# The prologue of a fused sketch-attention and feed-forward kernel: load order, k features and dummy matmuls rearranged

## The chip, the cores and the metric

The kernel runs on one core of a Trainium2 chip. The metric is the time of one execution on the device, in microseconds (us). The core has a matrix engine (TensorE, PE in the profile, with PEld for its weight loads), a vector engine (VectorE, DVE), an activation engine (ScalarE, ACT), a general engine (GpSimd, POOL) and a queue engine (SyncE, SP). DMA transfers are issued from SP's and ACT's queues here and run on 16 DMA engines. SBUF is the memory on the core; PSUM is the accumulator that TensorE writes.

## What is computed

Four batches of 1088 tokens with 4 heads of 32 go through a linear attention whose features are products of two small sketches, and the result through a feed-forward layer with a squared ReLU:

```python
def phi(x):                                   # S1, S2: 8 x 32
    a = np.einsum('rd,bhsd->bhsr', S1, x)
    b = np.einsum('rd,bhsd->bhsr', S2, x)
    return np.einsum('bhsi,bhsj->bhsij', a, b).reshape(*x.shape[:-1], r * r)   # 64 features
q_p, k_p = (phi(q), phi(k))
kv = np.einsum('bhsf,bhsd->bhfd', k_p, v)
z = np.sum(k_p, axis=2)
num = np.einsum('bhsf,bhfd->bhsd', q_p, kv)
den = np.einsum('bhsf,bhf->bhs', q_p, z)[..., None] + 1e-06
x = (num / den)                               # -> [4352 tokens, 128]
h = np.maximum(x @ w_in, 0.0)                 # 128 -> 2048
out = h * h @ w_out                           # 2048 -> 128
```

## The kernel before

The feed-forward layer works on stretches of 256 to 448 tokens of one batch. For each of the 16 blocks of 128 hidden features, TensorE makes `pg` (L562: w_in block by xT), ACT takes the ReLU `gt` (L571), ACT or VectorE squares it to `g` (L579, L581), and TensorE adds it into `po` (L600). The attention of the later stretches and batches is worked out in between. All of that, from the first `pg` on, is put in order by a planner (class `_Order`, with costs and due times): the costs and due times are fixed numbers in the code, and each engine runs its instructions in the planned order.

What stands ahead of the first `pg` is an order written out by hand, the prologue. It makes x for the first 256 columns of batch 0 (8 of the 34 token blocks of each head), for which it needs kv and z over all of batch 0's keys. Its steps, with their lines before:

- Loads. ACT's queue issues S1 and S2 into `s_nat` (L200, L201) and then v's parts 2 and 3; SP's queue issues k in two parts (token blocks 0 to 3 and 4 to 8 of each group, L164), the first 256 columns of q (L170), v's parts 0 and 1 (L177), and then w_in (L186), the rest of q and w_out (L191) in pieces. A v part fills 32 of the 128 partitions. A semaphore is shared by every eighth transfer, so the ninth waits until the first has landed.
- Dummies. `keep_warm(n)` (L633) issues n matmuls of 128x512 on constants into a tile that nobody reads. W0 to W5 are the counts at six places: 12, 2, 2, 2, 1, 1.
- Small constants. POOL makes `iden` (an identity, in a helper), `irep` (L238, four copies of parts of it), zeros in `vn` and `z`; VectorE makes `own_c`, `own_p` and zeros.
- Sketch matrices. VectorE transposes `s_nat` to `s_T` (L646); four copies by ACT and POOL put it block by block into `sf` (L648), others into `sq` (L650 to L657) and into further columns of `sf` (L684), which only the planned part reads.
- k features. VectorE transposes k in blocks of 32x32 to `kT` (L270). TensorE makes `kf` with the sketch in `sf` as the stationary operand and tokens moving (L294). The result has features on the partitions, so VectorE transposes it back to `fs` (L303), and then takes the products `kp` (L314).
- q features. `qT` (L276), four matmuls with `sq` into `x0` (L678), a copy `qb0` (ACT) and the product `qp0` (L694).
- kv. `kvp` (L368): 36 small matmuls (9 token blocks by 4 heads), accumulated in one PSUM tile, whose stationary operand is `kp` and whose moving operand is v and a column of ones. float32 matmuls show as two passes each.
- The end: `bd` (L701, masked kv), `den0` and `num0` (L718), and on VectorE `dT`, `dn`, `rd`, `bc` and `xT` (L725 to L735); beside that the copies of kv for the later stretches (`kvt`, `irep`, L411, L417). POOL casts w_in in four pieces of 512 columns (L710) for `pg`.

TensorE, VectorE, ACT and POOL each run their own instructions strictly in the order of the code, and so does each DMA queue.

Of the kernel before, what the change touches and what calls it, by code (L numbers as in the profile page):

```python
# [9 lines left out]
F32 = mybir.dt.float32  # L10
# [85 lines left out]
def kernel(  # L96
# [11 lines left out]
    nc = tc.nc  # L108
# [4 lines left out]
    SP = 128 * NT  # L113
# [4 lines left out]
    W0, W1, W2, W3, W4, W5 = 12, 2, 2, 2, 1, 1  # L118
# [24 lines left out]
    def sb(name, cols, dt=F32, rows=128):  # L143
        return cpool.tile([rows, cols], dt, tag=name, name=name)
# [24 lines left out]
    def load_q(eng, b, c0, c1):  # L169
        eng.dma_start(  # L170
            qn[b % 2][:, c0:c1],
            bass.AP(q.tensor, q.offset + b * H * S * D + c0, [[G * D, 128], [1, c1 - c0]]),
        )
# [28 lines left out]
    load_k(nc.sync, 0, 0, 4)  # L202
    load_k(nc.sync, 0, 4, 5)
# [3 lines left out]
    load_q(nc.sync, 0, 0, 256)  # L207
    load_v(nc.sync, 0, 0)
    load_v(nc.scalar, 0, 2)
    load_v(nc.sync, 0, 1)  # L210
    load_v(nc.scalar, 0, 3)
# [11 lines left out]
    iden = sb("iden", 128)  # L223
    make_identity(nc, iden[:])
# [5 lines left out]
    own_c, own_p, irep = sb("own_c", 32), sb("own_p", 2), sb("irep", 128)  # L230
# [4 lines left out]
    for h in range(H):  # L235
        r = slice(32 * h, 32 * h + 32)
        nc.vector.memset(own_c[r, 8 * h : 8 * h + 8], 1.0)
        nc.gpsimd.tensor_copy(  # L238
            _ap(irep, 32 * h, 32, 0, [[32, 4], [1, 32]]),
            _ap(iden, 32 * h, 32, 32 * h, [[0, 4], [1, 32]]),  # L240
        )

    nc.vector.memset(kT[:, S:SP], 0.0)
    nc.vector.memset(qT[:, S:SP], 0.0)
    for i in range(2):
        nc.gpsimd.memset(_ap(vn[i], 96, 32, 32 * (NT - 2), [[32 * NT, H], [1, 64]]), 0.0)
    nc.gpsimd.memset(vn[0][:, VC : VC + 32], 1.0)
    nc.gpsimd.memset(zs[1][:], 0.0)
    ones = vn[0][:, VC : VC + 32]
# [18 lines left out]
    def a_kT0(t0, n):  # L268
        p = 3 if t0 + n > NT - 2 else 4
        nc.vector.transpose(  # L270
            _ap(kT, 0, 128, 32 * t0, [[32 * NT, p], [1, 32 * n]]),
            _ap(kn[0], 0, 128, 32 * t0, [[32 * NT, p], [1, 32 * n]]),
        )
# [16 lines left out]
    def a_kf(t0, n, pool, tag):  # L290
        kf = pool.tile([128, 512], F32, tag=tag, name="kf")
        for x in range(2):
            for p in range(4):
                nc.tensor.matmul(  # L294
                    kf[32 * p : 32 * p + 32, 32 * n * x : 32 * n * x + 32 * n],
                    sf[:, 32 * x : 32 * x + 32],
                    kT[:, 32 * (NT * p + t0) : 32 * (NT * p + t0 + n)],
                )
        st["kf", t0] = kf

    def a_fs(t0, n):
        fs = wpool.tile([128, 64 * n], F32, tag="fs0", bufs=2, name="fs0")
        nc.vector.transpose(fs[:, :], st["kf", t0][:, 0 : 64 * n])  # L303
        st["fs0", t0] = fs
# [5 lines left out]
    def a_kp0(t0, n, g0, gn):  # L310

        fs = st["fs0", g0]
        o = 32 * (t0 - g0)
        nc.vector.tensor_tensor(  # L314
            out=_ap(st[0, "kp"], 0, 128, 256 * t0, [[64, 4 * n], [8, 8], [1, 8]]),
            in0=_ap(fs, 0, 128, o, [[8, 4 * n], [1, 8], [0, 8]]),
            in1=_ap(fs, 0, 128, o + 32 * gn, [[8, 4 * n], [0, 8], [1, 8]]),
            op=mult,
        )
# [325 lines left out]
    a_kT0(0, 4)  # L645
    nc.vector.transpose(s_T[:, :], s_nat[:, :])  # L646
    for h, eng in enumerate((nc.scalar.copy, nc.gpsimd.tensor_copy, nc.scalar.copy, nc.gpsimd.tensor_copy)):
        eng(_ap(sf, 32 * h, 32, 8 * h, [[32, 2], [1, 8]]), _ap(s_T, 0, 32, 0, [[8, 2], [1, 8]]))  # L648
    a_kf(0, 4, psf, "po")
# [6 lines left out]
    for h, eng in ((1, nc.scalar.copy), (2, nc.gpsimd.tensor_copy), (3, nc.scalar.copy)):  # L656
        eng(  # L657
            _ap(sq, 32 * h, 32, 64 * (h % 2), [[128, 2], [1, 64]]),
            _ap(sq, 0, 32, 0, [[128, 2], [1, 64]]),
        )  # L660
    a_kT0(4, 3)
    a_kT0(7, 2)
    a_qT(0, 0, 8)
    keep_warm(W1)
    a_kf(4, 5, psf, "po")
    a_fs(0, 4)
    new_kp(0)
    a_kp0(0, 4, 0, 4)
    a_fs(4, 5)
    a_kp0(4, 3, 4, 5)  # L670
    a_kp0(7, 2, 4, 5)
# [3 lines left out]
    for x in range(2):  # L675
        for y in range(2):
            r, o = slice(64 * y, 64 * y + 64), 512 * (2 * x + y)
            nc.tensor.matmul(x0[:, o : o + 256], sq[r, 128 * x : 128 * x + 128], qT[r, 0:256])  # L678
    qb0 = wpool.tile([128, 512], F32, tag="qb0", bufs=1, name="qb0")
    qp0 = wpool.tile([128, 512], F32, tag="qp0", bufs=1, name="qp0")  # L680
    nc.scalar.copy(_ap(qb0, 0, 128, 0, [[256, 2], [1, 256]]), banks(x0, 0, 0, 256))
    for h in range(H):
        eng = (nc.scalar.copy, nc.gpsimd.tensor_copy)[h % 2]
        eng(sf[32 * h : 32 * h + 32, 64:96], s_T[:, :])  # L684
    keep_warm(W2)
    st[0, "kvp"] = psf.tile([128, 512], F32, tag="pg", name="kvp")
    for t0, n in ((0, 4), (4, 3), (7, 2)):
        for t in range(t0, t0 + n):
            a_kv0(t)
        if t0 == 0:  # L690
            keep_warm(W3)
        elif t0 == 4:
            keep_warm(W4)
# [14 lines left out]
    nc.scalar.copy(st["kvt"][:, :], st[0, "kvp"][:, 0:128])  # L708
    for c in range(4):
        nc.gpsimd.tensor_copy(  # L710
            w_in[:, 512 * c : 512 * c + 512], w_in32[:, 512 * c : 512 * c + 512]
        )
    keep_warm(W5)
# [265 lines left out]
```

## Time and profile before

| | us |
|---|---|
| median of 5 runs | 197.35 (197.01 to 197.8) |
| the profiled execution | 197.2 |
| its span in the profile | 195.4 |
| first `pg` (start of the feed-forward stage) | 16.80 from the span's start |
| first `kvp` on TensorE | 10.18 |
| POOL's casts of w_in start | 9.39, 10.49, 12.82, 14.17 |

The profile is of one execution. Its times are counted from the span's start. "Idle before" is the time that the engine stood still just before an instruction, with what ended it. A line like `L314 DVE TENSOR_TENSOR kp<-fs 128x768` names the line of the code, the engine, the operation, the tile written and read, and the shape.

### The profile page before, as it was taken

The page shows a single profiled execution, that of the slowest core. Times are in us where ns is not written, and L with a number is a line of the kernel's source. Part 1 is how long each engine was busy: PE and PEld are TensorE (multiplying, and loading weights), DVE is VectorE, ACT ScalarE, POOL GpSimd, SP SyncE. Part 2 cuts the span into 40 slices and gives each one's busy share as a digit, 9 for nine tenths or more (in the row PEclk, how much of TensorE's full clock was granted, in tenths as well). Part 3 has the DMA queues.
Part 4 walks back from the last instruction along what each step waited for, and adds up shares of the span by engine and source line. Part 5 has one row for each costly group of instructions (what it writes and reads, how often), then busy time and mean ns, then how long its engine had stood idle before and what let it go on. Part 6 is the DMA issues. An engine that isn't in the chain of part 4 may idle for free.

```text
span 195.4 us, 4341 instructions
## 1 busy us (share of the span) xinstructions
PE 185.7 (95%) x1700; PEld 123.1 (63%) x1700; DVE 112.9 (58%) x253; ACT 147.1 (75%) x323; POOL 26.8 (14%) x121
## 2 busy tenths in 40 slices
PE   8796999999999999999999999999999999999990
PEld 2363676656656656756677667566677665666890
DVE  3768659983948569579462896694832322333300
ACT  3305887975958979779499897785899998888950
POOL 6240000004900000082000001940000000000000
PEclk9999999999999999999999999999999999999999
DMA  6999200010039220020018610020020010020200
GB/s 175 265 373 269 48 0 5 0 30 3 0 47 248 91 47 0 3 42 3 0 20 198 171 34 3 0 40 3 0 36 7 16 19 2 9 38 3 36 5 27
DMA packets 24604, 11.32 MB, mean 58 GB/s; under 512 B 17672, under 2 KB 23176, under 8 KB 24584
## 3 DMA queue, kind: packets, MB, share of 16 engines
q1 hardware_dynamic: 24132, 10.72, 22.4%
q10 hardware_dynamic: 452, 0.33, 0.7%
q8 instruction: 13, 0.21, 0.4%
q14 instruction: 7, 0.06, 0.1%
HBM read 8.82 MB, written 2.23 MB: 57 GB/s over the span
## 4 chain that ended last, share of the span: by engine, by line
PE 89%; DMA 3%; DVE 2%; ACT 2%; issue 1%; SPq 0%; DVEq 0%
PE po L600 56%; PE pg L562 17%; PE nd L484 3%; DMA qn<-in_q_dram 3%; PE nd L493 2%; PE kvp L386 2%; PE pol L595 2%; PE po L595 2%; PE kvp L368 1%; PE qc L283 1%; PE kc L283 1%; ACT gt L571 1%; ACT g L579 1%; DVE kp L314 1%; SPq L164 0%
## 5 line engine op out<-in xcount | busy, mean ns | idle before, releaser
L600 PE MATMUL po<-g,w_o 128*128 128x384 f32 (+3 forms) x352 | 137.3, 475 | 0.0
L562 PE MATMUL pg<-xT,w_in 128*128 128x384 f32 (+3 forms) x192 | 108.9, 575 | 1.9 <-DVE xT L735 1.2
L571 ACT ACTIVATE gt<-pg 128x384 f32<-128x384 f32 (+4 forms) x177 | 85.4, 490 | 27.0 <-PE pg L562 25.2
L600 PEld LDWEIGHTS po<-g,w_o 128*128 128x128 f32 x352 | 62.8, 189 | 20.1 <-issue 5.1
L579 ACT ACTIVATE g<-gt 128x384 f32<-128x384 f32 (+4 forms) x133 | 68.7, 530 | 2.9
L562 PEld LDWEIGHTS pg<-xT,w_in 128*128 128x128 f32 x192 | 35.8, 189 | 27.6 <-issue 7.3
L581 DVE TENSOR_TENSOR g<-gt 128x384 f32<-128x384 f32 (+3 forms) x44 | 24.5, 557 | 35.9 <-ACT gt L571 35.7
L435 POOL COPY kv<-kvt 32x64 f32<-32x64 f32 x48 | 12.4, 259 | 94.4 <-DVE kvt L404 92.5
L452 DVE STREAM_SHUFFLE qa<-qc 128x576 f32<-128x576 f32 (+2 forms) x20 | 11.7, 650 | 0.0
L467 DVE TENSOR_TENSOR qp<-qa,qb 128x576 f32<-128x576 f32 (+2 forms) x20 | 10.9, 604 | 0.0
L439 POOL COPY z<-kvt 32x16 f32<-32x16 f32 x48 | 10.1, 209 | 0.0
L604 DVE STREAM_TRANSPOSE oT<-po 128x384 f32<-128x384 f32 (+3 forms) x11 | 6.2, 566 | 4.0 <-PE po L600 4.0
L339 DVE TENSOR_TENSOR kp<-fs 128x576 f32<-128x576 f32 x12 | 8.5, 740 | 0.0
L509 DVE STREAM_TRANSPOSE dT<-nd 128x128 f32<-128x128 f32 (+2 forms) x8 | 2.2, 309 | 10.0 <-PE nd L493 10.0
L636 PE MATMUL warm<-const-bfloat16-1.0 128*128 128x512 bf16 x20 | 6.7, 462 | 0.8 <-PEq L963 0.8
L484 PE MATMUL nd<-qp,kv 32*32 32x288 f32 (+2 forms) x320 | 6.8, 353 | 0.0
L330 DVE STREAM_TRANSPOSE fs<-kc 128x576 f32<-128x576 f32 x6 | 4.3, 762 | 3.9 <-PE kc L283 3.9
L276 DVE STREAM_TRANSPOSE qT<-qn 128x576 f32<-128x576 f32 (+4 forms) x10 | 5.7, 607 | 1.4 <-DMA qn<-in_q_dram 1.4
L595 PE MATMUL pol<-w_o,g 128*128 128x128 f32 x32 | 6.2, 275 | 0.0
L595 PE MATMUL po<-w_o,g 128*128 128x128 f32 x32 | 6.2, 274 | 0.0
L484 PEld LDWEIGHTS nd<-qp,kv 32*32 32x32 f32 x320 | 3.8, 103 | 3.5 <-issue 2.1
L452 DVE STREAM_SHUFFLE qb<-qc 128x576 f32<-128x576 f32 (+2 forms) x10 | 6.0, 645 | 0.0
(83 smaller groups left out, 97.7 us busy)
## 6 DMA issues: line engine op xcount, KB each, us to landing
kn<-in_k_dram SPq DMA_DIRECT2D x3, 544.0 KB
qn<-in_q_dram SPq DMA_DIRECT2D x3, 544.0 KB, 7.7
vn<-in_v_dram SPq DMA_DIRECT2D x11, 144.0 KB, 6.1
out_dram<-oT SPq DMA_DIRECT2D x24, 48.0 KB, 1.8
w_in<-in_moe_w_in_dram SPq DMA_DIRECT2D x4, 256.0 KB, 5.0
w_o<-in_moe_w_out_dram SPq DMA_DIRECT2D x4, 256.0 KB, 5.1
out_dram<-oT SPq DMA_DIRECT2D x8, 56.0 KB, 1.8
qn<-in_q_dram SPq DMA_DIRECT2D x1, 416.0 KB, 6.7
```

The lines of the kernel that those rows point to most:

```text
L339: nc.vector.tensor_tensor(out=_ap(st[b, "kp"], 0, 128, 2 * o, [[64, NT], [8, 8], [1, 8]]), in0=_ap(fs, 0, 128, o, [[32, NT], [1, 8], [0, 8]]),
L435: nc.gpsimd.tensor_copy(_ap(st[b, "kv"], 32 * c, 32, 64 * h, [[32, E], [1, 32]]), _ap(st["kvt"], 32 * h, 32, 0, [[64, E], [1, 32]]),)
L439: nc.gpsimd.tensor_copy(_ap(zs[b % 2], 32 * c, 32, 64 * h + 8 * c, [[32, E], [1, 8]]), _ap(st["kvt"], 32 * h, 32, 32, [[64, E], [1, 8]]),)
L452: nc.vector.stream_shuffle(in_=banks(st[b, "qc", i0], 2 * x, 0, m), out=_ap(st[b, which, i0], 0, 128, 2 * m * x, [[m, 2], [1, m]]), mask=m ...
L467: nc.vector.tensor_tensor(out=st[b, "qp", i0, e][:, r], in0=st[b, f"qa{e}", i0][:, r], in1=st[b, "qb", i0][:, r], op=mult,)
L484: nc.tensor.matmul(nd[32 * h : 32 * h + 32, 512 * c + col : 512 * c + col + m], kv[r, o : o + 32], qp[r, m * h : m * h + m], start=(e == 0 ...
L562: nc.tensor.matmul(st["pg", u][:, n * i : n * i + n], w_in[:, 128 * (d0 + i) : 128 * (d0 + i) + 128], st[b, "xT"][:, c0 : c0 + n],)
L571: nc.scalar.activation(gt[:, 0:w], st["pg", u][:, 0:w], Relu)
L579: nc.scalar.activation(g2[:, 0:w], gt[:, 0:w], Square)
L581: nc.vector.tensor_tensor(out=g2[:, 0:w], in0=gt[:, 0:w], in1=gt[:, 0:w], op=mult)
L595: nc.tensor.matmul(po[x // 128][:, 0:128], g[:, x : x + 128], w, start=(d == 0), stop=(d == NB - 1),)
L600: nc.tensor.matmul(po[0][:, 0:n], w, g, start=(d == 0), stop=(d == NB - 1))
```

## The change

k's transpose now goes into a tile `kt0` of its own, in an order in which 128 tokens (one block of 32 from each of four groups) are neighbours; `kf` is made with these tokens as the stationary operand and `sf` (64 columns) moving, so that tokens come out on the partitions. ACT copies the second half of `kf` to `kb`, and the product `kp` reads the first half from PSUM and `kb` from SBUF. q's first columns are loaded between the two parts of k, and v's four parts all go into SP's queue. `s_T` is made ahead of `kt0`; its copies into `sf` are all POOL's. `iden`, `irep` and some zeros are made behind these copies. The q sketch matmuls stand between the k feature matmuls. The dummies are 11 at the start and none elsewhere. A copy of one column of `kp` on POOL stands ahead of the casts of w_in.

```diff
--- before.py
+++ after.py
@@ -115,7 +115,7 @@
     NB = 16
     GT, G2, LA = 4, 6, 3.5
     LU = 4
-    W0, W1, W2, W3, W4, W5 = 12, 2, 2, 2, 1, 1
+    W0, W1 = 11, 0
 
 
 
@@ -200,15 +200,13 @@
     nc.scalar.dma_start(s_nat[0:8, :], S1[:, :])
     nc.scalar.dma_start(s_nat[8:16, :], S2[:, :])
     load_k(nc.sync, 0, 0, 4)
+    load_q(nc.sync, 0, 0, 256)
     load_k(nc.sync, 0, 4, 5)
 
     zero_a = sb("zero_a", 8)
     nc.scalar.copy(zero_a[:, :], nc.const_aps.tensor(0.0, (128, 8), F32))
-    load_q(nc.sync, 0, 0, 256)
-    load_v(nc.sync, 0, 0)
-    load_v(nc.scalar, 0, 2)
-    load_v(nc.sync, 0, 1)
-    load_v(nc.scalar, 0, 3)
+    for p in range(4):
+        load_v(nc.sync, 0, p)
     load_wi(nc.sync, 0)
     load_wi(nc.sync, 1)
     load_q(nc.sync, 0, 256, S)
@@ -220,33 +218,26 @@
     load_wo(nc.sync, 3)
 
 
-    iden = sb("iden", 128)
-    make_identity(nc, iden[:])
 
 
     sf, sq = sb("sf", 96), sb("sq", 256)
     nc.vector.memset(sf[:, 0:64], 0.0)
     nc.gpsimd.memset(sq[:], 0.0)
-    own_c, own_p, irep = sb("own_c", 32), sb("own_p", 2), sb("irep", 128)
+    nc.gpsimd.memset(_ap(vn[0], 96, 32, 32 * (NT - 2), [[32 * NT, H], [1, 64]]), 0.0)
+    nc.gpsimd.memset(vn[0][:, VC : VC + 32], 1.0)
+    ones = vn[0][:, VC : VC + 32]
+
+    kt0 = sb("kt0", SP)
+    nc.vector.memset(_ap(kt0, 0, 128, 128 * (NT - 2) + 96, [[128, 2], [1, 32]]), 0.0)
+    own_c, own_p = sb("own_c", 32), sb("own_p", 2)
     nc.vector.memset(own_c[:], 0.0)
     nc.vector.memset(own_p[:], 0.0)
     for i in range(2):
         nc.vector.memset(own_p[64 * i : 64 * i + 64, i : i + 1], 1.0)
     for h in range(H):
-        r = slice(32 * h, 32 * h + 32)
-        nc.vector.memset(own_c[r, 8 * h : 8 * h + 8], 1.0)
-        nc.gpsimd.tensor_copy(
-            _ap(irep, 32 * h, 32, 0, [[32, 4], [1, 32]]),
-            _ap(iden, 32 * h, 32, 32 * h, [[0, 4], [1, 32]]),
-        )
-
+        nc.vector.memset(own_c[32 * h : 32 * h + 32, 8 * h : 8 * h + 8], 1.0)
     nc.vector.memset(kT[:, S:SP], 0.0)
     nc.vector.memset(qT[:, S:SP], 0.0)
-    for i in range(2):
-        nc.gpsimd.memset(_ap(vn[i], 96, 32, 32 * (NT - 2), [[32 * NT, H], [1, 64]]), 0.0)
-    nc.gpsimd.memset(vn[0][:, VC : VC + 32], 1.0)
-    nc.gpsimd.memset(zs[1][:], 0.0)
-    ones = vn[0][:, VC : VC + 32]
 
     mask_a = [[4 * e + l // 8 for l in range(32)] for e in range(E)]
     mask_b = [8 + l % 8 for l in range(32)]
@@ -268,8 +259,8 @@
     def a_kT0(t0, n):
         p = 3 if t0 + n > NT - 2 else 4
         nc.vector.transpose(
-            _ap(kT, 0, 128, 32 * t0, [[32 * NT, p], [1, 32 * n]]),
-            _ap(kn[0], 0, 128, 32 * t0, [[32 * NT, p], [1, 32 * n]]),
+            _ap(kt0, 0, 128, 128 * t0, [[32, p], [128, n], [1, 32]]),
+            _ap(kn[0], 0, 128, 32 * t0, [[32 * NT, p], [32, n], [1, 32]]),
         )
 
     def a_qT(b, i0, n):
@@ -289,32 +280,27 @@
 
     def a_kf(t0, n, pool, tag):
         kf = pool.tile([128, 512], F32, tag=tag, name="kf")
-        for x in range(2):
-            for p in range(4):
-                nc.tensor.matmul(
-                    kf[32 * p : 32 * p + 32, 32 * n * x : 32 * n * x + 32 * n],
-                    sf[:, 32 * x : 32 * x + 32],
-                    kT[:, 32 * (NT * p + t0) : 32 * (NT * p + t0 + n)],
-                )
-        st["kf", t0] = kf
-
-    def a_fs(t0, n):
-        fs = wpool.tile([128, 64 * n], F32, tag="fs0", bufs=2, name="fs0")
-        nc.vector.transpose(fs[:, :], st["kf", t0][:, 0 : 64 * n])
-        st["fs0", t0] = fs
+        for t in range(n):
+            nc.tensor.matmul(
+                _ap(kf, 0, 128, 32 * t, [[32 * n, 2], [1, 32]]),
+                kt0[:, 128 * (t0 + t) : 128 * (t0 + t) + 128],
+                sf[:, 0:64],
+            )
+        kb = wpool.tile([128, 32 * n], F32, tag="kb", bufs=3, name="kb")
+        nc.scalar.copy(kb[:, :], kf[:, 32 * n : 64 * n])
+        st["kf", t0] = kf, kb
 
     def new_kp(b):
 
         st[b, "kp"] = wpool.tile([128, 64 * NT * H], F32, tag="kp", name="kp")
 
-    def a_kp0(t0, n, g0, gn):
-
-        fs = st["fs0", g0]
-        o = 32 * (t0 - g0)
+    def a_kp0(t0, n):
+
+        kf, kb = st["kf", t0]
         nc.vector.tensor_tensor(
             out=_ap(st[0, "kp"], 0, 128, 256 * t0, [[64, 4 * n], [8, 8], [1, 8]]),
-            in0=_ap(fs, 0, 128, o, [[8, 4 * n], [1, 8], [0, 8]]),
-            in1=_ap(fs, 0, 128, o + 32 * gn, [[8, 4 * n], [0, 8], [1, 8]]),
+            in0=_ap(kf, 0, 128, 0, [[8, 4 * n], [1, 8], [0, 8]]),
+            in1=_ap(kb, 0, 128, 0, [[8, 4 * n], [0, 8], [1, 8]]),
             op=mult,
         )
 
@@ -642,11 +628,11 @@
 
     st["warm"] = psf.tile([128, 512], F32, tag="pg", name="warm")
     keep_warm(W0)
-    a_kT0(0, 4)
     nc.vector.transpose(s_T[:, :], s_nat[:, :])
-    for h, eng in enumerate((nc.scalar.copy, nc.gpsimd.tensor_copy, nc.scalar.copy, nc.gpsimd.tensor_copy)):
-        eng(_ap(sf, 32 * h, 32, 8 * h, [[32, 2], [1, 8]]), _ap(s_T, 0, 32, 0, [[8, 2], [1, 8]]))
-    a_kf(0, 4, psf, "po")
+    for h in range(H):
+        nc.gpsimd.tensor_copy(
+            _ap(sf, 32 * h, 32, 8 * h, [[32, 2], [1, 8]]), _ap(s_T, 0, 32, 0, [[8, 2], [1, 8]])
+        )
     nc.gpsimd.tensor_copy(
         _ap(sq, 0, 32, 0, [[8, 8], [1, 8]]), _ap(s_T, 0, 32, 8, [[0, 8], [1, 8]])
     )
@@ -658,39 +644,46 @@
             _ap(sq, 32 * h, 32, 64 * (h % 2), [[128, 2], [1, 64]]),
             _ap(sq, 0, 32, 0, [[128, 2], [1, 64]]),
         )
+    for h in range(H):
+        nc.gpsimd.tensor_copy(sf[32 * h : 32 * h + 32, 64:96], s_T[:, :])
+    iden, irep = sb("iden", 128), sb("irep", 128)
+    make_identity(nc, iden[:])
+    for h in range(H):
+        nc.gpsimd.tensor_copy(
+            _ap(irep, 32 * h, 32, 0, [[32, 4], [1, 32]]),
+            _ap(iden, 32 * h, 32, 32 * h, [[0, 4], [1, 32]]),
+        )
+    nc.gpsimd.memset(_ap(vn[1], 96, 32, 32 * (NT - 2), [[32 * NT, H], [1, 64]]), 0.0)
+    nc.gpsimd.memset(zs[1][:], 0.0)
+
+    a_kT0(0, 4)
+    a_qT(0, 0, 8)
     a_kT0(4, 3)
     a_kT0(7, 2)
-    a_qT(0, 0, 8)
-    keep_warm(W1)
-    a_kf(4, 5, psf, "po")
-    a_fs(0, 4)
-    new_kp(0)
-    a_kp0(0, 4, 0, 4)
-    a_fs(4, 5)
-    a_kp0(4, 3, 4, 5)
-    a_kp0(7, 2, 4, 5)
 
 
     x0 = att("x0")
-    for x in range(2):
+
+    def q0(x):
         for y in range(2):
             r, o = slice(64 * y, 64 * y + 64), 512 * (2 * x + y)
             nc.tensor.matmul(x0[:, o : o + 256], sq[r, 128 * x : 128 * x + 128], qT[r, 0:256])
+
+    new_kp(0)
+    a_kf(0, 4, psf, "po")
+    q0(0)
+    a_kf(4, 3, psf, "po")
+    q0(1)
+    a_kf(7, 2, psf, "pg")
     qb0 = wpool.tile([128, 512], F32, tag="qb0", bufs=1, name="qb0")
     qp0 = wpool.tile([128, 512], F32, tag="qp0", bufs=1, name="qp0")
     nc.scalar.copy(_ap(qb0, 0, 128, 0, [[256, 2], [1, 256]]), banks(x0, 0, 0, 256))
-    for h in range(H):
-        eng = (nc.scalar.copy, nc.gpsimd.tensor_copy)[h % 2]
-        eng(sf[32 * h : 32 * h + 32, 64:96], s_T[:, :])
-    keep_warm(W2)
+    keep_warm(W1)
     st[0, "kvp"] = psf.tile([128, 512], F32, tag="pg", name="kvp")
     for t0, n in ((0, 4), (4, 3), (7, 2)):
+        a_kp0(t0, n)
         for t in range(t0, t0 + n):
             a_kv0(t)
-        if t0 == 0:
-            keep_warm(W3)
-        elif t0 == 4:
-            keep_warm(W4)
     nc.vector.tensor_tensor(
         out=_ap(qp0, 0, 128, 0, [[256, 2], [1, 256]]), in0=banks(x0, 2, 0, 256),
         in1=_ap(qb0, 0, 128, 0, [[256, 2], [1, 256]]), op=mult,
@@ -706,11 +699,12 @@
         )
     st["kvt"] = wpool.tile([128, 128], F32, tag="kvt", name="kvt")
     nc.scalar.copy(st["kvt"][:, :], st[0, "kvp"][:, 0:128])
+
+    nc.gpsimd.tensor_copy(zero_a[:, 0:1], st[0, "kp"][:, 256 * NT - 1 : 256 * NT])
     for c in range(4):
         nc.gpsimd.tensor_copy(
             w_in[:, 512 * c : 512 * c + 512], w_in32[:, 512 * c : 512 * c + 512]
         )
-    keep_warm(W5)
     den0 = psf.tile([128, 512], F32, tag="po", name="den0")
     num0 = psf.tile([128, 512], F32, tag="pg", name="num0")
     for t_, x in ((den0, 1), (num0, 0)):
```

`a_kv0`, the end from `bd` to `xT` and the planned part are as they were.

## The prediction

> **What bounds the kernel now.** I read the page's busy times first, then the chain of waits, the SP queue's waits, and the groups of the first 17 us.
>
> ```profile
> PE 185.7 (95%) x1700; PEld 123.1 (63%) x1700; DVE 112.9 (58%) x253; ACT 147.1 (75%) x323; POOL 26.8 (14%) x121
> DMA  6999200010039220020018610020020010020200
> ```
>
> TensorE is busy for 95% of the span, and the change leaves that work alone. What can go is the time before the feed-forward stage starts, where the 16 DMA engines are busy (the nines). The chain of waits there (start, length, what):
>
> ```profile
> 1.80 5.21 DMA qn<-in_q_dram
> ...
> 7.03 0.45 DVE qT L276
> 7.48 0.34 DVE fs L303
> ...
> 7.84 1.23 DVE kp L314
> 9.06 0.44 DVE fs L303
> 9.50 0.68 issue
> 10.18 1.15 PE kvp L368 x32
> 11.34 0.54 PE warm L636 x2
> 11.87 0.85 PE kvp L368 x24
> 12.72 0.32 PE warm L636
> 13.04 0.64 PE kvp L368 x16
> ...
> 13.71 0.30 DVE bd L701
> ...
> 16.80 0.37 PE pg L562
> ```
>
> Vector work stands still until q lands at 7.01, then runs qT, fs, kp, fs. The 0.68 us of "issue" has no releaser named. The first `kvp` waits for all four v loads too, and the SP queue shows the last one landing (start, length, issue):
>
> ```profile
> 8.92 0.47 SPq L186 DMA_DIRECT2D w_in<-in_moe_w_in_dram  x1
> 10.11 0.93 SPq L191 DMA_DIRECT2D w_o<-in_moe_w_out_dram  x2
> ```
>
> The queue's waits put 0.7 us before the second line down to a v load, so the last v landed at about 10.1, and `kvp` starts at 10.15. From there TensorE alone sets the pace: 72 passes with five dummies among them to 13.68, then bd, and 3.09 us from bd to the first `pg`. Everything behind 16.80 has the same order in both kernels on every engine.
>
> The kp products (shape and count, busy, mean ns, idle before):
>
> ```profile
> L314 DVE TENSOR_TENSOR kp<-fs 128x768 f32<-128x768 f32 x1 | 1.3, 1285 | 0.0
> L314 DVE TENSOR_TENSOR kp<-fs 128x1024 f32<-128x1024 f32 x1 | 1.2, 1225 | 0.0
> L314 DVE TENSOR_TENSOR kp<-fs 128x512 f32<-128x512 f32 x1 | 1.1, 1092 | 0.0
> ```
>
> The smaller ones, which ran beside POOL's casts at 9.39 and 10.49, took as long as the largest, which ran alone. At 1.2 ns per column they would be 0.92 and 0.62 us.
>
> **Loads.** SP now issues k0 (256 KB), q (128), k1 (320), then v (3 x 144 and 112 KB); nothing competes from ACT but the two small S loads. SP's issues take 0.43 to 0.51 us each; v3 waits for k0's semaphore, so it goes out at about 3.65. k0 lands at 3.63 as before. k1's 320 KB landed 1.2 us later (275 GB/s), so q's 128 KB cost 0.48: q at 4.1, k1 at 5.3.
>
> The landing L of the last v is the unknown. Low end: v at the 329 to 352 GB/s of the windows from 2.5 to 4.0 us gives 557 kB / 343 = 1.6, L = 6.9. High end: on the SP queue v0 followed q (7.01) by 8.04 and v1 by 8.92, so 0.95 us for 144 KB, 3.6 for all, L = 8.9. In between: the four windows from 4 to 8 us, when mostly v flowed, moved 276, 238, 247 and 227 GB/s, mean 247, which gives 2.3 and L = 7.6. I take 8.0: the pair shared its engines with ACT's v loads, which makes it too slow, and the windows used two queues, which makes them too fast. The worst row is the 10.1 of today.
>
> The Trainium skill speaks against this part: "SBUF — State Buffer", section "Door 1: The DMA port swizzle", says that a transfer onto 32 partitions reaches only half of the 16 ports. By its 436 GB/s peak that is 218 GB/s for v, an estimate of 2.6 us and L = 7.9; no row here shows such a load by itself.
>
> **S and sf.** s_T goes ahead of kt0 on DVE. Today it ran at 4.26 without waiting, so S had landed by then. If it lands before k0: kt0 3.75 to 4.46 (0.71 row), and POOL's four sf copies (0.19 to 0.21 each, two of them ACT's until now) 3.8 to 4.65. If S lands only at 4.26, everything to kp0 is 0.65 later. kf0 then starts at 4.7, against 5.03; the eleven first dummies end at 4.7 (4.12 us for twelve), so they don't hold it.
>
> **k features.** 32 small matmul passes (0.64 and 0.75 us) become 18 passes with kt0 tokens as 128x128 weights and 64 columns moving. No row has that shape. Low end is `kvp`'s 34 ns a pass; high end is L595, 128x128 f32 weights and 128 columns, two passes in 0.22, so 110 ns. I take 110 (same weights): 0.9, 0.65 and 0.45 us for the groups of 4, 3 and 2 token blocks (kf0, kf1, kf2), plus 0.2 to the end. Both fs transposes (0.41, 0.51) leave DVE; three ACT copies kb (0.27 by the 128x128 row of L708) come in, and ACT is idle there. So:
>
> - kf0 4.7, done 5.8; kb 6.1; kp0 6.1 to 7.35
> - q0(0) on TensorE 5.6 to 6.25 (half of L678's 1.25), kf1 done 7.1, kb 7.35, kp1 to 8.3
> - q0(1) to 7.5, kf2 done 8.1, kb 8.3, kp2 8.35 to 8.95; qp0 (0.68) after qb0 (0.59) to 9.65
>
> DVE's kt1, kt2 (0.58, 0.34, from 5.3) and qT (0.45) lie under TensorE's work. kp0 has 0.65 us to spare before v at 8.0, and kp2 0.9 before the last `kvp` group needs it, so S late, or kp at its contended length (0.8 more for two), costs nothing or 0.1.
>
> **Casts held back.** POOL's small copy waits for the last kp, so nothing but the four casts queues behind it. The first cast runs at 9.0 or when w_in lands (9.39 today, at most about 0.5 later behind the joined v), 0.61 each: the first ends by 10.6, and `pg` needs it at 13.7. The last w_in landed at 14.17; its cast ends by 15.3, and the `pg` that reads it ran at 23.81, so at 20.8 now. iden, irep and the sf copies moved behind sq on POOL end at about 8.5; irep is needed at 12. Cost nothing. If that cover were gone, each 0.61 us cast would count.
>
> By "GPSIMD Engine Reference", section "Key points", of the Trainium skill, POOL contends with vector instructions that have two SBUF inputs. kp now reads kf from PSUM, so by that rule even an unheld cast would not slow it; the two rows above fit, but show only the old form.
>
> **Dummies.** Of 20, nine go. Four lay at 5.6 and 8.8 in idle time; three lie in the chain (0.54 + 0.32 us), and the last ends with bd, worth nothing.
>
> **Sum.** `kvp` starts at 8.0 instead of 10.15 (-2.15) and its 72 passes run 2.65 us instead of 3.5 (-0.86): bd at 10.68 instead of 13.71, -3.0 us. The 3.09 us to `pg` are unchanged, as are its later needs: the q rest landed by 11.5 (4.83 and 6.7; used at 13.9), the first w_o at 12.1 (7.02 and 5.1; used at 15.8), and the DMA share falls from 0.99 at 19 to 0.31 at 20 us, so the next k is in before its use at 22.8. The profiled execution took 197.2 (span 195.4 and 1.8 around it), so 194.2; it lies 0.15 under the median of 197.35, so 194.3.
>
> **Rivals.**
> - *Slower: v lands late on the one queue.* Batch 1's v loads, four in a row on SP, took 8.1 to 8.7 us from issue to landing. v3 issued at 3.65 would land at about 12.2, `kvp` end at 14.85, 1.15 later than now: 198.5. It decides from L above 11.05. Against: those stood behind twice as many bytes.
> - *The loads gain little.* q took 5.2 us to land, far more than its bytes explain. If k1 now lands at 7.0, L = 9.7 to 10.6 and bd comes at 12.4 to 13.3: 196.0 to 196.9, say 196.4. For: that row. Against: v2 on ACT landed beside q and is gone from there.
> - *The clock falls back* (the change then doesn't do what it says). The first dummies' weight loads came 0.43 us apart, later four came in 0.76:
>
> ```profile
> 3.29 0.15 PEld L636 LDWEIGHTS <-const-bfloat16-1.0 128*128 128x128 bf16 x1 [0.28 <-issue]
> 3.63 0.76 PEld L636 LDWEIGHTS <-const-bfloat16-1.0 128*128 128x128 bf16 x4 [0.20 <-issue]
> ```
>
> So TensorE can run at half speed. At that, `kvp` costs 2.65 more, den and `pg` 0.5: 197.4, no change. Against: the longest gap of TensorE today is 1.23 us, at 15.6, with nothing slower after it, and I expect no longer one.
>
> **How the numbers follow.** Mine 0.76, loads gain little 0.13, clock 0.04, slower 0.07. Measurements of this kernel tell 0.3% (0.6 us) from no change. Faster: 0.76 and most of 0.13, 0.87; same 0.06; slower 0.07. The low end is the kp floor: L = 6.9, kp2 at 8.95, last group 0.7, bd at 9.75, 3.95 us saved: 193.4, and 0.1 less for a quicker kf. The high end takes in L up to 10.1 (196.4).
>
> **What would show it.** Right: q's landing near 4.1; `kvp` starting at v's landing near 8 with kp0 done; 72 passes without a break; kp2 at 0.62 us; first `pg` at 13.8, rest of the timeline shifted alike. Wrong: `kvp` after 10, kp ending behind v, `pg` waiting for POOL, or the first `pg` early and the end not.

## The result, and the profile after

| | before | changed |
|---|---|---|
| median | 197.34 us (196.15 to 199.09, 79 runs) | 196.19 us (194.6 to 201.17, 44 runs) |
| ratio | | 0.993, 95% interval 0.9917 to 0.9944 |
| profiled execution, span | 197.2, 195.4 us | 196.26, 194.5 us |
| first `pg` | 16.80 us | 15.15 us |
| from the first `pg` to the end of the span | 178.6 us | 179.35 us |

The change gains 1.15 us by the medians, where 3.0 were forecast. Medians and ranges here take in every execution, while the ratios leave out those in a slower state (197.6 us or more for the changed kernel, 4 of its 44). Three later repeats of the same kernel, each beside the kernel before, gave ratios of 0.992, 0.9937 and 0.9928, with intervals that end at 0.9966 or below, so the gain is 1.2 to 1.7 us. The last two rows of the table say that two things went differently: the prologue became 1.65 us shorter and not 3.0, and 0.75 of that was lost again behind it.

First the prologue. SP's queue in the profile of the changed kernel (start, length, line, transfer issued) shows when earlier loads land, because from the ninth transfer on each issue needs an earlier one to have landed:

```profile
2.27 1.93 SPq L177 DMA_DIRECT2D vn<-in_v_dram  x4
...
6.94 0.38 SPq L191 DMA_DIRECT2D w_o<-in_moe_w_out_dram  x1
7.57 0.33 SPq L186 DMA_DIRECT2D w_in<-in_moe_w_in_dram  x1
8.36 0.38 SPq L191 DMA_DIRECT2D w_o<-in_moe_w_out_dram  x1
9.04 0.33 SPq L186 DMA_DIRECT2D w_in<-in_moe_w_in_dram  x1
9.53 0.93 SPq L191 DMA_DIRECT2D w_o<-in_moe_w_out_dram  x2
```

The issue at 6.94 waited for k's second part (k1), and the four behind it each for one part of v. So k1 landed at 6.93, and the last v at 9.53. VectorE's and TensorE's timelines (start, length, instruction, idle before and its releaser) say the same:

```profile
3.94 0.20 DVE L631 STREAM_TRANSPOSE s_T<-s_nat 32x32 f32<-32x32 f32 x1 [1.97 <-DMA s_nat<-in_S_dram]
4.08 0.66 DVE L261 STREAM_TRANSPOSE kt<-kn 128x512 f32<-128x512 f32 x1
4.67 0.39 DVE L267 STREAM_TRANSPOSE qT<-qn 128x256 f32<-128x256 f32 x1
5.42 1.16 PE L284 MATMUL kf<-sf,kt 128*128 128x64 f32 x8
6.50 0.70 PE L670 MATMUL x<-qT,sq 64*128 64x256 f32 x4
6.95 0.84 DVE L261 STREAM_TRANSPOSE kt<-kn 128x384 f32<-128x384 f32 x2 [1.89 <-DMA kn<-in_k_dram]
7.58 0.88 PE L284 MATMUL kf<-sf,kt 128*128 128x64 f32 x6 [0.37 <-DVE kt L261]
8.39 0.70 PE L670 MATMUL x<-qT,sq 64*128 64x256 f32 x4
9.03 0.66 PE L284 MATMUL kf<-sf,kt 128*128 128x64 f32 x4
9.61 2.32 PE L354 MATMUL kvp<-vn,kp 128*64 128x64 f32 x72
```

VectorE stands still for 1.89 us until k1 is in. TensorE's row of kf and q0 passes ends at 9.6, and v lands at 9.53: the two limits of `kvp` meet. `bd` follows at 11.98 (13.71 before), and 3.17 us later the first `pg`.

Then the 0.75 us. The stretches of the same execution (window, its length, busy time of PE, PEld, DVE, ACT and POOL with their instructions, granted clock, DMA share, GB/s):

```profile
15.00:16.00 1.00, 0.49 (x3) 0.31 (x3) 1.00 (x4) 0.42 (x2) 0.00 (x0) 0.99 1.01 385
16.00:17.00 1.00, 1.00 (x34) 0.76 (x34) 0.41 (x2) 0.97 (x3) 0.00 (x0) 0.50 1.10 253
17.00:18.00 1.00, 1.00 (x35) 0.74 (x4) 0.47 (x4) 0.97 (x3) 0.00 (x0) 0.50 1.11 221
18.00:19.00 1.00, 1.00 (x5) 0.82 (x4) 1.00 (x9) 0.74 (x2) 0.00 (x0) 0.50 1.07 218
19.00:20.00 1.00, 1.00 (x7) 0.95 (x7) 1.00 (x6) 0.62 (x2) 0.00 (x0) 0.80 1.03 253
```

The granted clock is half from 16.0 to 19.4 us. In the profile of before it was 1.00 throughout these windows:

```profile
17.00:18.00 1.00, 0.64 (x4) 0.36 (x3) 1.00 (x3) 0.78 (x3) 0.00 (x0) 1.00 1.17 226
18.00:19.00 1.00, 1.00 (x38) 0.76 (x36) 0.35 (x5) 0.97 (x4) 0.00 (x0) 1.00 1.02 211
```

The second pair of `pg` takes 0.79 us at half clock (changed, first) instead of 0.50 (before, second):

```profile
15.99 0.79 PE L548 MATMUL pg<-xT,w_in 128*128 128x256 f32 x2 [0.36 <-ACT gt L557]
```

```profile
17.63 0.50 PE L562 MATMUL pg<-xT,w_in 128*128 128x256 f32 x2 [0.36 <-ACT gt L571]
```

### The profile page after: what moved, and what is told of

Read it like the earlier page. It is cut to its first block, busy times and chain, and to the rows that moved or that the text cites. A ratio compares the mean times of both kernels' runs of the same rounds, so it can differ in the third digit from the quotient of the medians.

```text
span 194.5 us, 4301 instructions
## 1 busy us (share of the span) xinstructions
PE 186.0 (96%) x1677; PEld 125.3 (64%) x1677; DVE 111.2 (57%) x252; ACT 147.1 (76%) x322; POOL 27.9 (14%) x126
## 4 chain that ended last, share of the span: by engine, by line
PE 92%; DMA 3%; DVE 2%; issue 1%; SPq 0%; ACT 0%; DVEq 0%
PE po L586 57%; PE pg L548 18%; PE nd L470 3%; DMA kn<-in_k_dram 3%; PE nd L479 2%; PE kvp L372 2%; PE pol L581 2%; PE po L581 2%; PE qc L274 2%; PE kvp L354 1%; PE kc L274 1%; PE kf L284 1%; PE den L712 0%; PE x L670 0%; DVE kt L261 0%
## 5 line engine op out<-in xcount | busy, mean ns | idle before, releaser
L548 PE MATMUL pg<-xT,w_in 128*128 128x384 f32 (+3 forms) x192 | 110.1, 582 | 1.6 <-DVE xT L729 1.2
L548 PEld LDWEIGHTS pg<-xT,w_in 128*128 128x128 f32 x192 | 36.7, 193 | 27.0 <-issue 5.6
L425 POOL COPY z<-kvt 32x16 f32<-32x16 f32 x48 | 10.4, 217 | 0.0
L509 DVE STREAM_TRANSPOSE bc<-rd 128x576 f32<-128x576 f32 (+2 forms) x10 | 5.7, 610 | 0.2
```

Of the source, the lines that this page charges most:

```text
L425: nc.gpsimd.tensor_copy(_ap(zs[b % 2], 32 * c, 32, 64 * h + 8 * c, [[32, E], [1, 8]]), _ap(st["kvt"], 32 * h, 32, 32, [[64, E], [1, 8]]),)
L548: nc.tensor.matmul(st["pg", u][:, n * i : n * i + n], w_in[:, 128 * (d0 + i) : 128 * (d0 + i) + 128], st[b, "xT"][:, c0 : c0 + n],)
```

## The experiments

All edits but one are made to the changed kernel; line numbers are those of each run's own kernel, and `...` stands for lines left out. In the expectations, "before" is the kernel before the change.

### The half clock: dummies in the gaps

`keep_warm` gets a target and a first column, and its matmuls fill the two gaps of TensorE that lie ahead of the first `pg`: two between `kvp` and `den`, seven between `num` and `pg`.

```diff
+    keep_warm(2, 256, den0, 256)
     for t_, x in ((den0, 1), (num0, 0)):
...
     nc.vector.transpose(dT0[:, :], den0[:, 0:256])
+    keep_warm(7, 256, den0, 256)
```

> The changed kernel with nine dummy matmuls of 256 columns put into gaps in which TensorE waits anyway: two between kvp and den, seven between x and the first pg. Theory A (the clock: with no dummies behind the start, TensorE's share of work in the 3.4 us before the first pg is too low, and its clock is halved from about 16.0 to 19.4 us in most executions): granted clock 1.0 from 15 to 25 us, first pg near 15.2 as in the changed kernel, time 195.2 (1.0 less than the changed kernel's 196.2), and little scatter. Theory B (the 0.75 us between first pg and the end went elsewhere, to loads or to the order of the feed-forward start): still about 196.2, clock or not.

> The kernel with dummies in the two gaps once more, beside the changed kernel on one chip. Its first profile had no drop of the clock and the first pg at 15.17, but its median was 196.28, not 195.2. Theory A (the clock is what costs 0.75 to 1 us): mean granted clock 0.994 or more in nearly all executions, and 0.5 to 1.0 less time than the changed kernel beside it. Theory B (the drop hides in waits of the feed-forward start, and the scatter is that of the loads): mean clock as high, time the same as the changed kernel within 0.3.

Measured: 196.28 us (ratio 0.9964, 0.9939 to 0.9989) and, repeated beside a control, 196.1 us (0.9935, 0.9908 to 0.9963); the control, which is the changed kernel unaltered, had 195.8 (0.992, 0.9893 to 0.9947).

> The changed kernel itself, on the same chip and in the same rounds as the filled gaps and k in one transfer, because those are compared with it. 196.2 by its earlier runs; one or two drops of the granted clock to one half in most executions (mean clock 0.99 or 0.983), none in the fastest.

The dummies do hold the clock: 23 of 24 executions had a mean granted clock of 0.994 or more (one half-clock stretch of 3.4 us in 194 takes it to 0.991 or less), against 5 of 12 in the control. But they bought no time: the control's five executions of 0.994 or more (called undisturbed from here on) had a median span of 193.5 us, the undisturbed ones with dummies 194.4 and 194.3. In the second profile the first `pg` came at 14.72, and 1.3 us were lost against the control's profile at 107 us, where batch 3's k landed late:

```profile
107.01 1.37 DVE L256 STREAM_TRANSPOSE kT<-kn 128x576 f32<-128x576 f32 x2 [3.26 <-DMA kn<-in_k_dram]
```

In the control this wait was 1.1 us. That load has no margin, whatever the prologue does. The wait was 3.1 us in the third kernel with such dummies (further down) and 1.1 to 1.8 us in the other sixteen profiles, the first one with dummies among them. So in two of three profiled executions the dummies come with this loss, and in those two it is at least as large as what they save. Why the load comes late there is not shown.

What the half clock itself costs can be read from the time between the first `pg` and the end of the span. It is 178.5 to 178.6 us in the eight profiles without these dummies that keep the full clock at the start of that stage, and 179.3 to 179.6 in the six that have one stretch of 3.4 us at half clock beginning between 16 and 17 us: 0.7 to 1.1 us more. With dummies it is 178.5, or 180.0 and 179.8 where batch 3's k was late.

The half clock is not new either. Over all batches, 43 of 97 executions of before fell under 0.994, and 49 of 80 of the changed kernel (its 44 runs and three controls). Like with like, the changed kernel's median spans are 193.4 to 193.6 undisturbed and 194.4 to 194.7 disturbed, those of before in four batches 195.0 to 195.3 and 195.8 to 196.2. In the three batches that hold both kernels the gain is 1.5 to 1.6 us undisturbed and 1.2 to 1.7 disturbed, around the 1.65 seen at the first `pg`. By an estimate from these numbers the more frequent half clock takes only about 0.2 us from the mean, (49/80 - 43/97) x 1.1.

### Which part brings the gain: fewer dummies alone, new loads taken back

The first edit is to before, the second to the changed kernel.

```diff
-    W0, W1, W2, W3, W4, W5 = 12, 2, 2, 2, 1, 1
+    W0, W1, W2, W3, W4, W5 = 12, 0, 0, 0, 0, 0
```

```diff
     load_k(nc.sync, 0, 0, 4)
-    load_q(nc.sync, 0, 0, 256)
     load_k(nc.sync, 0, 4, 5)
...
-    for p in range(4):
-        load_v(nc.sync, 0, p)
+    load_q(nc.sync, 0, 0, 256)
+    load_v(nc.sync, 0, 0)
+    load_v(nc.scalar, 0, 2)
+    load_v(nc.sync, 0, 1)
+    load_v(nc.scalar, 0, 3)
```

> The kernel before with its twelve first dummies and none of the eight later ones. Theory A (clock): the chain from kvp to bd is 0.86 us shorter, first pg near 15.95, but the clock is halved for about 3.4 us in many executions, which gives most of it back: 196.5 with a full clock, 197.3 to 197.7 with a halved one, so a median of about 197.3 and a wider scatter than before. Theory B (the dummies only cost time): 196.5, granted clock 1.0 throughout.

> The changed kernel with the loads in the order and on the queues of the kernel before (both parts of k, then q; v parts 2 and 3 from ACT). If the new load order is what brings the first pg forward: k1 lands at 4.8, q at 7.0, the last v at 10.1, kvp starts at 10.15 and runs 2.35, first pg at 15.7, 0.5 later than with the new order; time about 196.7. If the order of loads is worth nothing: first pg at 15.2 again, 196.2. If the single queue is a loss: first pg before 15.0.

Measured: 196.63 us (ratio 0.9976, 0.9951 to 1.0001) with the eight later dummies gone, first `pg` at 15.73; 196.58 us (0.995, 0.9924 to 0.9977) with the old loads, first `pg` at 15.99. The `kvp` rows of the two:

```profile
10.28 2.32 PE L368 MATMUL kvp<-vn,kp 128*64 128x64 f32 x72 [1.51 <-DMA vn<-in_v_dram]
```

```profile
10.39 2.32 PE L356 MATMUL kvp<-vn,kp 128*64 128x64 f32 x72
```

Both start at 10.3 to 10.4, where before started at 10.18, and run their 72 passes in 2.32 us without a break. So fewer dummies in the chain are worth 1.07 us at the first `pg` and no other part of the change is needed for that. The new k features bring nothing while the loads are the old ones (q landed at 7.04, VectorE makes kt1 behind qT, and `kvp` starts when TensorE's kf and q0 passes end, v being in at 10.06). The new loads are worth the rest: 0.6 (15.73 to 15.15) to 0.8 (15.99 to 15.15) in these profiles. That split rests on single executions: the first `pg` of the unaltered changed kernel came anywhere from 14.76 to 15.32 in four profiles, and the times do not tell the old loads (0.995) from the new (0.993).

### Why k1 is late: another queue, one transfer, nothing behind it

k1 is issued from ACT's queue, behind the S loads:

```diff
+    load_k(nc.scalar, 0, 4, 5)
     load_k(nc.sync, 0, 0, 4)
     load_q(nc.sync, 0, 0, 256)
-    load_k(nc.sync, 0, 4, 5)
```

> The changed kernel with the second part of k issued by ACT behind S1 and S2 instead of third on SP's queue. Theory Q (one queue in order can't feed the 16 engines at the start: they were 63 to 90% busy from 3.5 to 5.0 us): both queues run, k1 lands by 5.5 instead of 6.93, and the share of the DMA engines from 3.5 to 5.0 us goes to about 1.0; kf1 at 6.6, the last v by 9.0, first pg near 14.6, 0.5 us less. Theory R (704 KB have landed by 7.0 whatever the order or the queue): k1 at 6.9 again, first pg at 15.2.

All of batch 0's k goes in one transfer:

```diff
-    load_k(nc.sync, 0, 0, 4)
+    load_k(nc.sync, 0)
     load_q(nc.sync, 0, 0, 256)
-    load_k(nc.sync, 0, 4, 5)
```

> The changed kernel with k of batch 0 in one transfer of 128 rows of 4352 bytes instead of two of 512 and 640 byte pieces. Theory P (the engines are held up by the number of pieces: k takes 1024 of the 1152 packets before v): k whole lands by 5.0, the rate from 2.5 to 5.0 us is above 330 GB/s without the dip at 3.5, the last v lands by 8.7, first pg near 14.4, time 195.4. Theory R (the transfers behind k decide): k whole lands at 6.5 to 7, kf0 starts 1.5 later than now, first pg at 15.2 or later.

v is issued only once k1 has landed and is transposed, and the later SP loads behind v:

```diff
-    for p in range(4):
-        load_v(nc.sync, 0, p)
...
     a_kT0(7, 2)
+    for p in range(4):
+        nc.vector.tensor_copy(vn[0][32 * p : 32 * p + 32, 0:1], kt0[32 * p : 32 * p + 32, 512:513])
+    for p in range(4):
+        load_v(nc.sync, 0, p)
...
```

> The changed kernel with v and all later loads of SP issued only after k1 has been transposed, so that nothing is behind k1 in the queue. Theory R (k1's landing is late because the engines work on v while some still hold pieces of k1): k1 lands at 5.3, as worked out from its bytes. Theory Q (k1 itself comes late: it is issued at 1.8 and moves slowly): k1 lands at 6.5 to 6.9 with nothing behind it. The whole is slower in either case, first pg near 18, because v starts at 6 to 8.

Measured: k1 from ACT's queue is worse, 199.96 us (ratio 1.0107, 1.0049 to 1.0165; four executions, 197.52 to 201.9). The profile is of the slowest of them: k1 landed at 8.16, TensorE stood idle for 1.58 us, and `kvp` ran at half clock (4.05 us). By the times a second queue isn't the remedy. k in one transfer is worse too, 198.97 us (1.0102, 1.0062 to 1.0142). k was in by 4.92, but the two S loads of 1 KB landed only at 5.38, kf0 came at 6.58, and the clock was half from 9.0. With nothing behind k1 (196.76 us, one execution) the row is:

```profile
5.67 0.58 DVE L250 STREAM_TRANSPOSE kt<-kn 128x384 f32<-128x384 f32 x1 [0.53 <-DMA kn<-in_k_dram]
```

Against 6.42 to 7.12 in the seven profiles with v behind it, k1 lands 0.75 to 1.45 us earlier, within 0.4 us of the forecast's 5.3. What remains shows in the flow. The windows of this execution, of the changed kernel and of before, in that order:

```profile
3.50:4.00 0.50, 0.50 (x2) 0.15 (x1) 0.00 (x0) 0.00 (x0) 0.00 (x0) 1.00 0.83 70
4.00:4.50 0.50, 0.50 (x2) 0.15 (x1) 0.47 (x2) 0.18 (x1) 0.19 (x1) 1.00 0.71 198
```

```profile
3.50:4.00 0.50, 0.50 (x2) 0.15 (x1) 0.06 (x1) 0.00 (x0) 0.00 (x0) 1.00 0.63 152
4.00:4.50 0.50, 0.50 (x2) 0.15 (x1) 0.50 (x2) 0.24 (x1) 0.25 (x2) 1.00 0.86 210
```

```profile
3.50:4.00 0.50, 0.50 (x3) 0.20 (x2) 0.37 (x1) 0.00 (x0) 0.21 (x1) 1.00 1.15 352
4.00:4.50 0.50, 0.50 (x4) 0.20 (x2) 0.42 (x2) 0.05 (x1) 0.00 (x0) 1.00 0.93 277
```

70 and 198 GB/s, where before moved 352 and 277. The same dip stands in the changed kernel's four profiles (152 and 210, 119 and 122, 133 and 175, 99 and 154) and in none of the three with the old loads, where k1 is directly behind k's first part (277 to 352).

The packets in the traces can be told apart by size: k1 moves in pieces of 640 bytes, v in pieces of 1152 and 896. They show v overtaking k1 although it was issued later. In the changed kernel's profile above, v's first piece starts at 4.65 and k1's last ends at 6.14, and by then 252 of v's 544 KB have moved. In the seven profiles with k1 third and v behind it this is 138 to 252 KB; with k1 on ACT's queue, where it landed at 8.16, it is 498 KB; with nothing behind it, none. With the old loads it is 48 KB (k1 in at 4.84) and twice 122 KB (5.58 and 5.75).

### The casts

```diff
-    nc.gpsimd.tensor_copy(zero_a[:, 0:1], st[0, "kp"][:, 256 * NT - 1 : 256 * NT])
```

> The changed kernel without the small POOL copy that holds the casts of w_in behind the last kp. My theory: kp reads kf from PSUM, so casts beside it cost it nothing: kp stays at 1.2, 0.94 and 0.69 us (it was so beside POOL's irep copies), the first cast moves from 10.85 to about 8.6 to 9.5, the time is that of the changed kernel within 0.3%. Rival (the casts slow kp, as the two rows of the kernel before suggest): kp1 or kp2 goes to 1.1 to 1.2 us, and where kp2's end sets the last kvp group, bd is 0.1 to 0.5 us later.

Measured: 196.32 us (ratio 0.9942, 0.991 to 0.9973); the control beside it 195.61 (0.9937, 0.9907 to 0.9966): no difference.

> The changed kernel again, as the control for the three beside it: 195.8 to 196.3, 0.992 to 0.995 of the kernel before, first pg at 14.7 to 15.2.

```profile
9.74 1.25 POOL L704 CAST w_in<-w_in 128x512 fp32r<-128x512 f32 x2 [0.58 <-DMA w_in<-in_moe_w_in_dram]
...
9.96 0.69 DVE L300 TENSOR_TENSOR kp<-kf,kb 128x512 f32<-128x512 f32 x1 [0.24 <-ACT kb L290]
```

The freed cast runs over the last kp, and kp takes the same 0.69 us as without it. Before, the kp of that size took 1.09 us beside a cast. In this execution the kp that reads one operand from PSUM isn't slowed, so holding the casts back is worth nothing; the new kp made it needless.

### k1 ahead of q, and the S copies on two engines

```diff
     load_k(nc.sync, 0, 0, 4)
-    load_q(nc.sync, 0, 0, 256)
     load_k(nc.sync, 0, 4, 5)
+    load_q(nc.sync, 0, 0, 256)
...
     a_kT0(0, 4)
-    a_qT(0, 0, 8)
     a_kT0(4, 3)
     a_kT0(7, 2)
+    a_qT(0, 0, 8)
...
     a_kf(0, 4, psf, "po")
-    q0(0)
     a_kf(4, 3, psf, "po")
-    q0(1)
     a_kf(7, 2, psf, "pg")
+    q0(0)
+    q0(1)
```

> The changed kernel with k's second part ahead of q's columns in SP's queue, kt made ahead of qT on VectorE, and on TensorE the three kf groups ahead of the two q0 pairs. Theory P (place in the queue): k1 was late because it went out third, issued at 1.8 behind q, into the thin DMA windows at 3.5 to 4.5 us; second in line it lands at 4.85 to 5.2 (4.84 in the kernel before) in spite of the same bytes behind it. The last v keeps its bytes ahead of it and lands at 9.0 to 9.5. With S in by 4.2, kf0 starts at 5.1 to 5.4, TensorE's 18 kf and 8 q0 passes take 4.1 us without a break, kvp starts at 9.2 to 9.5 and the first pg comes at 14.7 to 15.0: 0 to 0.4 us below the changed kernel beside it, so k1 by itself was worth little and v is what binds. Theory T (traffic behind it): k1 lands at 6.0 or later again, kvp at 9.6 or later. Third case: the two S loads land behind the larger part, at 5.2 to 5.4 (as in the kernel before with 12 dummies and in the one with k whole); then kf0 starts at 6.1, kvp at 10.2, pg at 15.7, 0.6 to 0.9 us above the changed kernel.

> The kernel with k's second part ahead of q and all sf copies on POOL, once more, one look. Theory P: k1 at 4.8 to 5.2, S at about 4.2, kf0 at 5.4, kvp at 8.8 to 9.2. Theory C: S or k1 late again in some way, as in the first look (S 5.23, k1 6.85).

And with the four sf copies shared out as before:

```diff
-    for h in range(H):
-        nc.gpsimd.tensor_copy(
+    for h, eng in enumerate((nc.scalar.copy, nc.gpsimd.tensor_copy, nc.scalar.copy, nc.gpsimd.tensor_copy)):
+        eng(
```

> As the kernel with k's second part ahead of q, and the four copies of s_T into sf go to ACT and POOL in turn, as in the kernel before, instead of all to POOL. Two copies in turn on two engines take 0.42 us (row of the kernel before) instead of 0.88, so kf0 starts 0.4 us earlier. If TensorE's chain of kf and q0 passes sets kvp's start, kvp and pg move by 0.3 to 0.4 us against the run without the split; if v's landing sets it, by 0 to 0.1.

> The kernel with k's second part ahead of q and the sf copies split, once more, beside the changed kernel. If k1's place in the queue sets its landing (theory P), k1 lands near 5.1 again and kvp starts at 8.7 to 9.0, first pg 14.3 to 14.6. If chance sets it (theory C; the same loads gave 6.85 and 5.10 in two executions), it lands anywhere from 4.8 to 6.9 and kvp starts at 8.7 to 9.9. Time by P: 0.4 to 0.8 us below the changed kernel beside it; by C: 0 to 0.4 us.

The same with the dummies of the first experiment, and the control:

> The same with 2 dummies of 256 columns between kvp and den and 7 between den and the first pg. Nearly all executions keep the full clock after the first pg. If the 0.75 us of half clock is what hides the gain, the time is 0.7 us below that of the same kernel without these dummies; if the dummies give back what they save, as in the two looks at them in the changed kernel, the two are within 0.3 us.

> The changed kernel again, as the control: 195.6 to 196.3, k1 at 6.4 to 7.1, first pg at 14.7 to 15.3.

Measured, each with the control of its batch (S and k1: landing; `kvp` and first `pg`: start, in the profiled execution, in us):

| | median us | ratio (95%) | S | k1 | `kvp` | first `pg` |
|---|---|---|---|---|---|---|
| k1 ahead of q | 196.19 | 0.9919 (0.9887 to 0.9952) | 5.23 | 6.85 | 9.81 | 15.36 |
| sf split too | 195.55 | 0.9901 (0.9864 to 0.9938) | 4.13 | 5.10 | 8.74 | 14.29 |
| control | 195.61 | 0.9937 (0.9907 to 0.9966) | 3.78 | 7.12 | 9.79 | 15.32 |
| k1 ahead of q, again | 196.11, one execution | | 4.60 | by 5.4 | 9.01 | 15.00 |
| sf split too, again | 194.92 | 0.9866 (0.9821 to 0.9912) | 3.95 | by 4.7 | 8.08 | 13.62 |
| the same with dummies | 195.43 | 0.9893 (0.9856 to 0.9931) | 4.32 | by 5.1 | 8.95 | 14.40 |
| control | 195.91 | 0.9928 (0.9897 to 0.9959) | 4.29 | 6.63 | 9.30 | 14.91 |

("By" where the engine came to it later and found it landed.) With k1 second in the queue it landed by 5.4 in four of these five executions, and by 5.75 in the three profiles with the old loads; third, and with v behind it, it never landed before 6.42. In the four, at most 41 KB of v had overtaken it. In the fifth, with 6.85, it was 297 KB, so a second place does not rule the overtaking out, and chance takes part as well. In that execution S was late too. The dip is gone in all five; of the 194.92 us kernel:

```profile
3.50:4.00 0.50, 0.50 (x2) 0.15 (x1) 0.05 (x1) 0.00 (x0) 0.00 (x0) 1.00 1.15 348
4.00:4.50 0.50, 0.50 (x3) 0.20 (x2) 0.50 (x2) 0.30 (x2) 0.19 (x1) 1.00 1.10 315
```

Its timeline, against that of the changed kernel shown above:

```profile
4.09 1.38 DVE L261 STREAM_TRANSPOSE kt<-kn 128x512 f32<-128x512 f32 x3
...
4.89 2.19 PE L284 MATMUL kf<-sf,kt 128*128 128x64 f32 x18
7.01 1.14 PE L668 MATMUL x<-qT,sq 64*128 64x256 f32 x8
8.08 2.32 PE L354 MATMUL kvp<-vn,kp 128*64 128x64 f32 x72
...
13.62 0.47 PE L548 MATMUL pg<-xT,w_in 128*128 128x256 f32 x2 [1.22 <-DVE xT L727]
```

The three kt run without a break, so k1 had landed by 4.7. All 18 kf passes and the q passes follow without a gap, and v, without the dip ahead of it, is in by 8.1. In this execution, the quickest of the three profiles, `kvp` starts where the forecast had put it, and the first `pg` comes 0.2 us before the forecast's 13.8. By the ratios of two batches (0.990 and 0.987) this version beats the kernel before. Against the changed kernel it is ahead by 0.4% and 0.6% of these ratios, but the intervals overlap and the medians of the first batch differ by 0.06 us only, so that gain isn't shown by the times alone. Like with like its median spans are the lower ones in both batches, undisturbed (192.6 and 192.4, one and three executions, against 193.6 and 193.5) and disturbed (193.7 and 193.9 against 194.6 and 194.4). The dummies on top hold the clock in six of six executions and again give no time.

## Why the prediction was wrong, point by point

- **The step that failed: "q at 4.1, k1 at 5.3", and from it L = 8.0.** It priced k1 by its bytes at the rate of the old order. q's place was right (in by 4.67 at the latest), but k1 landed at 6.93. The runs show two reasons: the v parts issued behind k1 overtake part of it (252 KB of v had moved by k1's last piece; without them k1 landed 0.75 to 1.45 us earlier), and with q second the flow falls to 70 to 217 GB/s from 3.5 to 4.5. The two go together: with k1 second there is no dip, and in four of five executions k1 was through before much of v moved, so their shares can't be added up. L came out as 9.53. The rival "the loads gain little" had k1 at 7.0 and L at 9.7 to 10.6, `bd` at 12.4 or later; measured 9.53 and 11.98. So this rival is the one that came, with a little less loss than it said. That its time, 196.4, is so near the measured 196.19 is partly luck, as the passes were quicker than it had them and the half clock took some of that back.
- **v's own rate is not what the 2.6 us from k1's landing to the last v show.** 544 KB in that time would be 214 GB/s. But 413 of v's 544 KB had moved by then, by the sizes of the packets, and the windows from 7.0 to 9.5 moved 237, 234, 302, 317 and 395 GB/s, 0.74 MB together, more than all of v: v finished among the loads behind it, as k1 had. The Trainium skill's "SBUF — State Buffer", section "Door 1: The DMA port swizzle", led to an estimate of 218 GB/s and 2.6 us for v. The changed kernel's trace can't confirm it. Where v flowed alone (nothing behind k1) its pieces took 2.5 us from first to last, close to the estimate, but the windows from 8.0 to 9.5 moved 300, 290 and 257 GB/s, so 218 was no ceiling for the four parts together. The forecast's reason for v3's issue time was misread, at no cost: by the order of the transfers the ninth waits for S1, not for k0, and SP issued the four parts without a break.
- **S and kf0.** S came at 3.94, between the two cases, and kf0 at 5.42 instead of 4.7: POOL's four copies ended at 5.09 instead of 4.65, and the eleven dummies, which took 4.85 us where twelve had taken 4.12, ran on to kf0. With the copies on two engines kf0 began at 4.89 once and at 5.26 and 5.42 in the two other profiles.
- **kf at 110 ns a pass** held. With the forecast's 0.2 us to the end the groups were to take 1.1, 0.85 and 0.65 us; they took 1.16, 0.88 and 0.66, and all 18 passes in a row 2.19. What moved TensorE's chain is its start, 5.42 for 4.7, and the 0.37 us that it waited for kt1: its kf and q0 rows, 4.1 us together, ended beside v's landing.
- **kp at 1.2, 0.92 and 0.62 us**: 1.19, 0.94 and 0.69. The casts cost nothing, as forecast, and the cover that was named for them wasn't even needed.
- **72 passes at 2.65 us**: 2.32, better by 0.33. The dummies' share, forecast at 0.86, was 1.07 us at the first `pg` by the run without them, more than the loads brought.
- **3.09 us from `bd` to `pg`**: 3.17.
- **The clock rival** was dismissed because the longest gap, 1.23 us, had been harmless. The argument was wrong, as one profile can't show it: with the same gap of 1.22 us the clock fell in the changed kernel's profile and stayed full in its first control's, and by the mean clock it fell in 44% of the executions of before and 61% of those of the changed kernel. Its cost was small, because it fell behind the prologue (0.75 us in the profiled execution, some 0.2 us between the kernels). The Trainium skill's "TensorE: Matmul & The Clock Gate", Part 1, describes a free-running activity window of about 3.4 us; the 3.4 us at half clock and the chance in it agree. Its rule of no idle gap over about 3.4 us (section "HAM oscillation — how this bites in real kernels") does not cover it: none in the changed kernel's profile was over 1.3 ahead of the drop.

In sum: 3.03 us forecast at `bd`, less 1.61 for `kvp`'s start (9.61 for 8.0), plus 0.33 for the passes, makes 1.75; measured 1.73. Of these, 1.65 reached the first `pg`, and the half clock behind it took 0.75 in the profiled execution.

## What to carry to other kernels

Price a transfer by its place in the queue and by what is issued behind it, not by its own bytes alone, and look in the windows for a flow that thins out. Here it paid to put the large part that the chain needs next directly behind the first, and a small one after it. Before building on one profile's clock, look at the clocks of many executions.

## What was not expected of the hardware

- A small transfer (q, 128 KB) in second place goes with a dip to 70 to 217 GB/s for about 1 us in all nine profiles that have it behind k's first part; in the nine with k1 or all of k ahead of it there is none in the same windows (267 GB/s and more). Why the engines run short there is open.
- The 1 KB S loads landed anywhere from 3.8 to 5.4 us, latest behind k in one transfer.
- A cast on POOL can hold up a tiny VectorE instruction that works in SBUF alone, while kp, with an operand in PSUM, wasn't touched. In the second run of "k1 ahead of q", `dn` took 0.61 us instead of 0.17, exactly as long as the cast beside it, and the first `pg` came 0.45 us later after `bd` than in the changed kernel's profile:

```profile
12.97 0.61 POOL L705 CAST w_in<-w_in 128x512 fp32r<-128x512 f32 x1 [1.63 <-DMA w_in<-in_moe_w_in_dram]
12.99 0.61 DVE L721 TENSOR_SCALAR dn<-dT 128x8 f32<-128x8 f32 x1
```
